# Two weight pieces loaded behind the first inputs, and a new order in the first slots, of an attention and two-layer kernel

## The chip, the cores and the metric

The kernel runs on one core of a Trainium2 chip. The metric is device time in microseconds (us) for one execution. TensorE (PE in the rows) multiplies, VectorE (DVE), ScalarE (ACT) and GpSimd (POOL) do elementwise work, SyncE (SP) issues nearly all transfers. TensorE's clock has two levels, 1.2 and 2.4 GHz; the rows give the granted share, 0.50 or 1.00.

## What is computed

Banded attention over 4 batches of 8 heads, then two feed-forward layers over 2304 tokens, all in float32. The layer weights come in as int64 views, of which the kernel makes float32 numbers.

```python
scores = scale * np.matmul(q, k.transpose(0, 1, 3, 2))
scores = np.where(masks[None, :, :, :], scores, -1000000000.0)
attn = np.exp(scores - np.max(scores, axis=-1, keepdims=True))
attn = attn / (np.sum(attn, axis=-1, keepdims=True) + 1e-09)
x = np.matmul(attn, v)            # then heads side by side: 2304 x 512
h = x @ w_in                      # first layer, 512 -> 2048
g = np.maximum(h, 0.0) + alpha * np.minimum(h, 0.0)
x = g @ w_out
h = x @ w_in2                     # second layer
g = np.where(h >= 1, h, np.where(h <= -1, 0.0, (h + 1) ** 2 / 4))
out = g @ w_out2
```

## The kernel before

**Splits.** Every product is made of three float32r matmuls: each operand is split into a high part (`hi`) and the rest (`lo`). `two` (lines 325 to 327) does it: ScalarE copies the high part (line 326), GpSimd or VectorE subtracts (line 327). The split of a w_in piece is called `wr`, that of a w_out piece `woh` and `wol`, that of x `xv`, that of g `gh` and `gl` (lines 660 and 666).

**Weight pieces.** A piece (layer, f, part) is one of 16 chunks f of w_in (part 0, tile `wi`) or w_out (part 1, `wo`; pieces that are kept for later are `wf`). `w_load` (line 271) loads 512 KB of it into a staging tile `st`, of which there are five. `w_make` turns it into float32 by three VectorE instructions (lines 320, 321 and 314), and when the third is done the staging tile is free for the next load. `conv(k)` hands out k of these instructions, so it says where they stand in VectorE's queue; `more` issues loads as long as a staging tile is free. `pend_l` and `pend_w` are the lists of pieces still to load and to make. `w_cut` splits each finished w_in piece.

**Attention.** 24 groups, six to a batch. The groups of batch 0 run ahead of everything, in a loop over i: scores (PE, lines 172 and 180), maximum and subtraction (DVE, lines 189 and 190), exp (ACT, line 192), a transpose of the previous group (line 211, evacuated as `pT`, line 213), its values (line 204), its normalisation (DVE, lines 228 to 230) and the output transpose of the one before (line 237, evacuated to `XA`, line 255). Groups 6 and up are spread over the slots of the first three tiles by `attention_point` (lines 141 to 164 for scores, 211 to 237 for the rest).

**Tiles and slots.** The first layer's tokens are tiles (0, 0) to (0, 3), the second layer's (1, 0) to (1, 2). Tiles (0, 0), (0, 1), (0, 2) and (1, 2) go in slots, one for each f: `f_h` makes h on TensorE (lines 513 to 515, twelve matmuls), `f_g` the activation (ACT line 650, DVE line 653, ACT line 660), `f_cut` the split of g, and `one_y` an earlier chunk's product with w_out into y (lines 688 to 690, twelve matmuls). h has two PSUM buffers, so h of chunk f + 2 needs that g of chunk f has been read. Slots are numbered by k from 0; the h of chunks 0 and 1 of tile (0, 0) stand between the last groups of batch 0, part by part, as x becomes ready.

**Pairs.** Tiles (0, 3), (1, 0) and (1, 1) have 1024 tokens and use Strassen's seven products. In the second half of such a tile, 16 steps of twelve matmuls each finish y for its second half of tokens, with `gx` loaded back from memory. Meanwhile `more_x` makes the next tile's seven inputs (22 operations of `x_seven`: sums called `room` on VectorE, and splits), `p_weights` the next tile's first weights (a split, four sums `ss`, further splits), and, in the first pair only, steps 3 to 10 make eight w_out pieces, three instructions each.

**What sets the order.** The order is written out by hand: each engine runs its instructions in the order in which the code issues them, and waits in that order.

Of the kernel before, what the change touches and what calls it, by code (L numbers as in the profile page):

```python
# [26 lines left out]
NF = DFF // P  # L27
# [31 lines left out]

EARLY = (3, 6)  # L60
READY = 12
# [26 lines left out]
def attention_then_two_ffns(ctx: ExitStack, tc: tile.TileContext, a0, aqk, av, w1i, w1o, w2i, w2o, alpha, masks, ident, out):  # L88
# [623 lines left out]
    with tc.manual_schedule(), ExitStack() as late:  # L712
# [22 lines left out]
        for i in range(NGB):  # L735
# [4 lines left out]
            if i == 1:  # L740
                nc.sync.dma_start(mask[:, 2 * GS:], masks[:, 2 * GS:])
        nc.sync.dma_start(al, alpha)
        nc.scalar.activation(half, half, AF.Exp, scale=0.0)
        nc.scalar.activation(half, half, AF.Copy, scale=0.5)
# [24 lines left out]
        def conv(k):  # L769

            for _ in range(k):
                if not todo and pend_w and pend_w[0] in cv:
                    todo.extend(w_make(*pend_w.pop(0)))
                if todo:
                    todo.pop(0)()
                    if not todo:
                        more()
# [8 lines left out]
        for i in range(NGB):  # L786
# [10 lines left out]
            w_cut()  # L797
            if i in FIRST:
                conv(3)
            if i == 3:  # L800
                x_split(n0, 0, True)

                nc.gpsimd.memset(qk[0], 0.0)
                hold = False
                a_load_qk(NGB)
                w_load(*pend_l.pop(0))
                w_load(*pend_l.pop(0))
                a_load_v(NGB)
                more()
# [17 lines left out]
        w_cut()  # L827
        conv(3)
        nc.vector.tensor_scalar(al, al, -1.0, 1.0, ALU.mult, ALU.add)
# [68 lines left out]
        def slot(n, f, k):  # L898
            nn = after_n[n]
            if k != 1:  # L900
                split_pending()
            w_cut()
            if n == LAST and f == NF - 1:
# [4 lines left out]
            if early:  # L908
                one_y()
            if n == PLAIN[0] and f == NF - 1:  # L910
                pend_l.extend(pend_2)
                pend_w.extend(pend_2)
# [8 lines left out]
            else:  # L921
                ops = 0
            attention_point()
            b0, b1 = BEFORE[n[0]]
            g = f_g(n, f, lambda: conv(min(ops, b0)))
            ops -= min(ops, b0)
            first_ops = min(ops, b1) if k else 1
            conv(first_ops)
            f_cut(n, f, g)
            if k == 0:  # L930
                wo_split((n, 0), f)
            w_cut()
            ahead = 2 if n == PLAIN[0] else 3
# [83 lines left out]
        for q, n in enumerate(PAIRS):  # L1017
# [41 lines left out]
            for i, f in enumerate(SECOND):  # L1059
# [12 lines left out]
                f_y((n, 1), f)  # L1072
                more_x(2)
                if nn in PAIRS:
# [122 lines left out]
```

## Time and profile before

| | us |
|---|---|
| median of three runs | 860.86 (858.82 to 861.88) |
| the profiled execution | 859.94 |
| its span | 858.2 |
| TensorE busy | 837.3 (98%) |
| VectorE busy | 554.5 (65%) |
| ScalarE busy | 428.8 (50%) |
| GpSimd busy | 481.9 (56%) |
| mean granted clock of TensorE | 0.992 |

The span is the time from the first to the last instruction of the profiled execution. In rows of the timeline, what stands in brackets at the end is how long the engine stood idle before the instruction, and which instruction's end released it. "issue" is a wait for nothing that the profile shows. An engine's busy time says little here of what bounds it: TensorE's idle time is 21 us in 858, and each piece of it stands in a place of its own.

### The profile page before, as it was taken

The numbers are of one execution on the slowest core, as the hardware profiler recorded it, in microseconds if no ns is written. First come the engines' busy times: TensorE is split into PE (matmuls) and PEld (weight loads), VectorE is DVE, ScalarE is ACT, GpSimd is POOL, SyncE is SP. The second block draws the span as 40 slices with busy tenths as digits, with TensorE's granted clock in tenths as the row PEclk, the third lists the DMA queues.
The fourth block names the chain that finished last, engine by engine and source line by source line (L and its number), as shares of the span: only waits on it lengthen the run. The fifth ranks groups of instructions, "written<-read, shape, count | busy, mean of one in ns | idle before, by whom it ended". The sixth has DMA issues, their size and how long they took to land.

```text
span 858.2 us, 14266 instructions
## 1 busy us (share of the span) xinstructions
PE 837.3 (98%) x5328; PEld 688.7 (80%) x5330; DVE 554.5 (65%) x911; ACT 428.8 (50%) x803; POOL 481.9 (56%) x411
## 2 busy tenths in 40 slices
PE   6899999999999999999998999999999999999998
PEld 4677777998777778888886888888888888888898
DVE  4788786666877576776678677776418677640143
ACT  3444444665534565555444556464335545453365
POOL 2365545777444677767346676763662332346486
PEclk8899999999999999999999999999999999999999
DMA  7787653764661025444287735333935553548220
GB/s 298 236 245 224 198 166 113 223 216 124 194 187 50 1 74 179 141 152 167 99 330 270 275 131 203 141 156 112 344 123 188 201 195 126 173 139 302 70 79 25
DMA packets 54980, 147.45 MB, mean 172 GB/s; under 512 B 5632, under 2 KB 13440, under 8 KB 54912
## 3 DMA queue, kind: packets, MB, share of 16 engines
q1 hardware_dynamic: 54624, 146.39, 50.3%
q8 instruction: 42, 0.69, 0.3%
q14 instruction: 26, 0.21, 0.1%
q10 hardware_dynamic: 288, 0.16, 0.1%
HBM read 101.97 MB, written 44.56 MB: 171 GB/s over the span
## 4 chain that ended last, share of the span: by engine, by line
PE 88%; DVE 6%; ACT 2%; issue 2%; DMA 1%; POOL 1%; SPq 0%; ACTq 0%; DVEq 0%
PE y L688 14%; PE y L690 14%; PE y L689 14%; PE h_ps L546 9%; PE h_ps L544 9%; PE h_ps L545 9%; PE h_ps L513 5%; PE h_ps L515 4%; PE h_ps L514 4%; PE o_ps L222 2%; PE s_ps L148 1%; DVE room L452 1%; PE t_ps L211 1%; PE x_ps L237 1%; DVE w_ps L321 1%
## 5 line engine op out<-in xcount | busy, mean ns | idle before, releaser
L327 POOL TENSOR_TENSOR wol<-wo,woh 128x512 fp32r<-128x512 f32 x153 | 200.0, 1314 | 86.5 <-ACT woh L326 86.2
L688 PE MATMUL y<-gh,wol 128*128 128x512 f32 (+1 forms) x444 | 164.0, 369 | 0.6 <-POOL wol L327 0.6
L690 PE MATMUL y<-gl,woh 128*128 128x512 f32 (+1 forms) x444 | 160.2, 361 | 0.0
L689 PE MATMUL y<-gh,woh 128*128 128x512 f32 (+1 forms) x444 | 160.2, 361 | 0.0
L327 POOL TENSOR_TENSOR wr<-wb,wr 128x512 fp32r<-128x512 f32 x60 | 77.7, 1295 | 128.3 <-ACT wr L326 128.3
L546 PE MATMUL h_ps<-xv,wr 128*128 128x512 f32 x336 | 130.8, 389 | 0.0
L545 PE MATMUL h_ps<-xv,wr 128*128 128x512 f32 x336 | 130.8, 389 | 0.0
L544 PE MATMUL h_ps<-xv,wr 128*128 128x512 f32 x336 | 130.7, 389 | 0.0
L326 ACT ACTIVATE woh<-wo 128x512 fp32r<-128x512 f32 x153 | 93.6, 626 | 71.8 <-PE y L690 52.2
L327 POOL TENSOR_TENSOR wr<-wi,wr 128x512 fp32r<-128x512 f32 x50 | 64.5, 1290 | 98.4 <-ACT wr L326 98.2
L688 PEld LDWEIGHTS y<-gh,wol 128*128 128x128 f32 x444 | 83.7, 189 | 16.7 <-POOL wol L327 2.3
L513 PE MATMUL h_ps<-xv,wr 128*128 128x512 f32 (+1 forms) x256 | 90.7, 354 | 3.8 <-DVE g L653 2.0
L690 PEld LDWEIGHTS y<-gl,woh 128*128 128x128 f32 x444 | 83.6, 188 | 13.4
L689 PEld LDWEIGHTS y<-gh,woh 128*128 128x128 f32 x444 | 83.8, 189 | 12.2
L514 PE MATMUL h_ps<-xv,wr 128*128 128x512 f32 (+1 forms) x256 | 87.0, 340 | 0.2 <-DVE xv L327 0.2
L515 PE MATMUL h_ps<-xv,wr 128*128 128x512 f32 (+1 forms) x256 | 87.0, 340 | 0.0
L558 ACT ACTIVATE g<-g,half 128x512 f32<-128x512 f32 x64 | 44.7, 723 | 72.1 <-DVE g L557 70.9
L688 PE MATMUL y<-gx,wol 128*128 128x512 f32 x192 | 75.5, 393 | 2.7 <-POOL wol L327 2.7
L689 PE MATMUL y<-gx,woh 128*128 128x512 f32 x192 | 75.3, 392 | 0.0
L690 PE MATMUL y<-gx,woh 128*128 128x512 f32 x192 | 75.3, 392 | 0.0
L545 PEld LDWEIGHTS h_ps<-xv,wr 128*128 128x128 f32 x336 | 63.1, 188 | 13.2
L544 PEld LDWEIGHTS h_ps<-xv,wr 128*128 128x128 f32 x336 | 63.1, 188 | 13.2
(122 smaller groups left out, 1513.7 us busy)
## 6 DMA issues: line engine op xcount, KB each, us to landing
gd<-XA SPq DMA_DIRECT2D x42, 512.0 KB, 3.5
gx<-gd SPq DMA_DIRECT2D x42, 512.0 KB, 5.9
wb<-whole SPq DMA_DIRECT2D x30, 512.0 KB, 4.8
st<-w1i SPq DMA_DIRECT2D x16, 512.0 KB, 5.0
st<-w1o SPq DMA_DIRECT2D x16, 512.0 KB, 5.2
st<-w2i SPq DMA_DIRECT2D x16, 512.0 KB, 4.8
st<-w2o SPq DMA_DIRECT2D x16, 512.0 KB, 4.8
kept<-wr SPq DMA_DIRECT2D x16, 512.0 KB, 2.7
```

Of the source, the lines that this page charges most:

```text
L326: nc.scalar.activation(hi, src, AF.Copy)
L327: low_on.tensor_tensor(lo, src, hi.bitcast(F32), ALU.subtract)
L513: nc.tensor.matmul(ps[:, :w], r[:, 1, cs], x[:, 0, xs], start=(c == 0), stop=False)
L514: nc.tensor.matmul(ps[:, :w], r[:, 0, cs], x[:, 1, xs], start=False, stop=False)
L515: nc.tensor.matmul(ps[:, :w], r[:, 0, cs], x[:, 0, xs], start=False, stop=(c == NC - 1))
L544: nc.tensor.matmul(o, w[:, 1, cs], x[:, 0], start=start and m == 0, stop=False, skip_group_check=not start)
L545: nc.tensor.matmul(o, w[:, 0, cs], x[:, 1], start=False, stop=False, skip_group_check=not start)
L546: nc.tensor.matmul(o, w[:, 0, cs], x[:, 0], start=False, stop=m == 1, skip_group_check=not start)
L558: nc.scalar.activation(t, t, AF.Square, bias=half, scale=0.5)
L688: nc.tensor.matmul(o, wl[:, cs], gh[:, :w], start=(i == 0), stop=False)
L689: nc.tensor.matmul(o, wh[:, cs], gh[:, :w], start=False, stop=False)
L690: nc.tensor.matmul(o, wh[:, cs], gl[:, :w], start=False, stop=(i == NF - 1))
```

## The change

Four things are moved; no instruction that computes is added or left out.

- The pieces (0, 2, 0) and (0, 0, 1) are loaded straight behind batch 0's inputs and alpha, ahead of the first transfers of batch 1 (`qk`, `vz`), and are made after the values of groups 3 and 4 (i = 4 and 5).
- In the first slots, VectorE's g of chunk 0 and 1 stands ahead of more of the pieces' instructions (`EARLY`, `b0`, `first_ops`); `w_cut` moves behind `f_g` in every slot of the plain tiles, and in slot 2 the split of the w_out piece stands behind the attention's instructions.
- The second layer's pieces are put on the list of loads two slots earlier, at f = 13 of tile (0, 0).
- In the second half of the first pair, the 22 input operations are given out as three in each of the first three steps, one in each of steps 3 to 10, and three after that, instead of two in each step.

```diff
--- before.py
+++ after.py
@@ -57,7 +57,7 @@
 
 FIRST = (0, 2)
 
-EARLY = (3, 6)
+EARLY = (2, 3)
 READY = 12
 BEFORE = ((1, 1), (1, 3))
 
@@ -740,6 +740,8 @@
             if i == 1:
                 nc.sync.dma_start(mask[:, 2 * GS:], masks[:, 2 * GS:])
         nc.sync.dma_start(al, alpha)
+        for _ in range(2):
+            w_load(*pend_l.pop(0))
         nc.scalar.activation(half, half, AF.Exp, scale=0.0)
         nc.scalar.activation(half, half, AF.Copy, scale=0.5)
         nc.gpsimd.memset(qk[1][:D, QK:], 0.0)
@@ -795,7 +797,7 @@
             if i >= 1:
                 e_values(i - 1)
             w_cut()
-            if i in FIRST:
+            if i in FIRST or i >= 4:
                 conv(3)
             if i == 3:
                 x_split(n0, 0, True)
@@ -803,8 +805,6 @@
                 nc.gpsimd.memset(qk[0], 0.0)
                 hold = False
                 a_load_qk(NGB)
-                w_load(*pend_l.pop(0))
-                w_load(*pend_l.pop(0))
                 a_load_v(NGB)
                 more()
             if i == 4:
@@ -825,7 +825,7 @@
         f_h(n0, 1, (2,))
         x_split(n0, 3)
         w_cut()
-        conv(3)
+        conv(1)
         nc.vector.tensor_scalar(al, al, -1.0, 1.0, ALU.mult, ALU.add)
         a_load_qk(NGB + 1)
         a_load_v(NGB + 1)
@@ -897,9 +897,10 @@
 
         def slot(n, f, k):
             nn = after_n[n]
-            if k != 1:
+            if k not in (1, 2):
                 split_pending()
-            w_cut()
+            if k > 1 and (n, f) not in wt:
+                w_cut()
             if n == LAST and f == NF - 1:
                 wo_split((n, 0), f)
             if k > 1 or n == LAST:
@@ -907,8 +908,9 @@
             early = f < 2 and k > 1
             if early:
                 one_y()
+            if n == PLAIN[0] and f == NF - 3:
+                pend_l.extend(pend_2)
             if n == PLAIN[0] and f == NF - 1:
-                pend_l.extend(pend_2)
                 pend_w.extend(pend_2)
             if n in PLAIN[:2] and f >= NF - NC:
                 x_split(nn, f - NF + NC, n == PLAIN[1])
@@ -921,15 +923,18 @@
             else:
                 ops = 0
             attention_point()
+            if k == 2:
+                split_pending()
             b0, b1 = BEFORE[n[0]]
-            g = f_g(n, f, lambda: conv(min(ops, b0)))
-            ops -= min(ops, b0)
-            first_ops = min(ops, b1) if k else 1
+            b0 = min(ops, b0) if k else 0
+            g = f_g(n, f, lambda: conv(b0))
+            ops -= b0
+            first_ops = min(ops, b1 if k else 3)
+            w_cut()
             conv(first_ops)
             f_cut(n, f, g)
             if k == 0:
                 wo_split((n, 0), f)
-            w_cut()
             ahead = 2 if n == PLAIN[0] else 3
             for i in range(1, ahead + 1):
                 if f + i < NF:
@@ -1070,7 +1075,7 @@
                         pend_y += [((n, 1), x) for x in SECOND[i:]]
                         break
                 f_y((n, 1), f)
-                more_x(2)
+                more_x(2 if q else 1 if 3 <= i < 11 else 3)
                 if nn in PAIRS:
                     if i in (5, 13):
                         w_base(nn[0], i // 13)
```

On VectorE, from the last split parts of group 5 to g of chunk 0 (line 653): `wi` is piece (0, 2, 0) before and (0, 3, 0) after, `wo` is (0, 0, 1) before and (0, 1, 1) after, `w_ps` the next piece in PSUM, `al` alpha. Before:

```order
L321 SCALAR_TENSOR_TENSOR wi<-st,wi 128x512
L314 SCALAR_TENSOR_TENSOR wi<-st,wi 128x512
L327 TENSOR_TENSOR xv<-XA,xv 128x512
L320 TENSOR_SCALAR wo<-st 128x512
L321 SCALAR_TENSOR_TENSOR wo<-st,wo 128x512
L314 SCALAR_TENSOR_TENSOR wo<-st,wo 128x512
L829 TENSOR_SCALAR al<-al 128x16
L320 TENSOR_SCALAR w_ps<-st 128x512
L653 SCALAR_TENSOR_TENSOR g<-g,al,h_ps 128x512
```

The same place after:

```order
L321 SCALAR_TENSOR_TENSOR wi<-st,wi 128x512
L314 SCALAR_TENSOR_TENSOR wi<-st,wi 128x512
L327 TENSOR_TENSOR xv<-XA,xv 128x512
L320 TENSOR_SCALAR wo<-st 128x512
L829 TENSOR_SCALAR al<-al 128x16
L653 SCALAR_TENSOR_TENSOR g<-g,al,h_ps 128x512
L321 SCALAR_TENSOR_TENSOR wo<-st,wo 128x512
```

Two instructions of the w_out piece and one of the next now stand behind g; the six of the two early pieces stand further up, between the normalisations of groups 3, 4 and 5.

On ScalarE, slots 0 and 1 of tile (0, 0), from gh of chunk 0 to pT of group 6. Before:

```order
L660 ACTIVATE gh<-g 128x512
L326 ACTIVATE woh<-wo 128x512
L326 ACTIVATE wr<-wi 128x512
L164 ACTIVATE s<-s 128x384
L650 ACTIVATE g<-h_ps 128x512
L660 ACTIVATE gh<-g 128x512
L326 ACTIVATE woh<-wo 128x512
L326 ACTIVATE wr<-wi 128x512
L213 ACTIVATE pT<-t_ps 128x384
```

After:

```order
L660 ACTIVATE gh<-g 128x512
L326 ACTIVATE woh<-wo 128x512
L164 ACTIVATE s<-s 128x384
L650 ACTIVATE g<-h_ps 128x512
L660 ACTIVATE gh<-g 128x512
L213 ACTIVATE pT<-t_ps 128x384
L326 ACTIVATE woh<-wo 128x512
```

Both splits of w_in pieces are gone from between, and pT stands ahead of the second woh.

On ScalarE, steps 8 and 9 of the first pair's second half (`wb` and `ss` are the next tile's weights and their sums). Before:

```order
L326 ACTIVATE woh<-wo 128x512 x2
L326 ACTIVATE xv<-room 128x512 x2
L326 ACTIVATE wr<-wb 128x512
L326 ACTIVATE woh<-wo 128x512
L326 ACTIVATE xv<-room 128x512
L326 ACTIVATE wr<-ss 128x512
```

After:

```order
L326 ACTIVATE xv<-XA 128x512
L326 ACTIVATE woh<-wo 128x512
L326 ACTIVATE wr<-wb 128x512
L326 ACTIVATE woh<-wo 128x512
L326 ACTIVATE wr<-ss 128x512
L326 ACTIVATE woh<-wo 128x512
```

The three splits of `room` no longer stand ahead of the weights' splits. TensorE's instructions stand in the same order before and after.

## Rows read from the trace of the kernel before

**Rows 1.** The page's first part: busy time, share of the span, instructions.

```profile
PE 837.3 (98%) x5328; PEld 688.7 (80%) x5330; DVE 554.5 (65%) x911; ACT 428.8 (50%) x803; POOL 481.9 (56%) x411
```

**Rows 2.** TensorE's timeline: start, duration, line, operation; in brackets the wait.

```profile
20.71 0.66 PE L204 MATMUL o_ps<-e_in,pT 64*32 64x65 f32 x25 [2.49 <-issue]
...
39.58 0.53 PE L513 MATMUL h_ps<-xv,wr 128*128 128x512 f32 x1 [1.95 <-DVE g L653]
...
48.69 0.87 PE L222 MATMUL o_ps<-vz,pT 128*32 128x130 f32 x24 [1.46 <-ACT pT L213]
...
149.99 0.39 PE L513 MATMUL h_ps<-xv,wr 128*128 128x256 f32 x1 [1.70 <-POOL wr L327]
...
272.35 0.55 PE L237 MATMUL x_ps<-idt,o 128*128 128x128 f32 x3 [0.55 <-DVE s L152]
...
279.61 0.87 PE L222 MATMUL o_ps<-vz,pT 128*32 128x130 f32 x24 [0.85 <-ACT pT L213]
...
464.81 0.50 PE L688 MATMUL y<-gx,wol 128*128 128x512 f32 x1 [2.30 <-POOL wol L327]
...
471.06 0.50 PE L688 MATMUL y<-gx,wol 128*128 128x512 f32 x1 [0.40 <-POOL wol L327]
```

**Rows 3.** Stretches: busy PE, PEld, DVE, ACT, POOL; granted clock, DMA share, GB/s.

```profile
14.00:16.00 2.00, 1.56 (x98) 1.23 (x97) 0.74 (x3) 0.34 (x1) 0.00 (x0) 0.99 1.03 405
20.00:22.00 2.00, 1.29 (x51) 0.82 (x59) 0.50 (x3) 1.30 (x4) 1.14 (x1) 0.50 0.05 8
40.00:42.00 2.00, 2.00 (x6) 1.56 (x5) 1.93 (x5) 0.90 (x3) 1.82 (x2) 0.50 1.00 318
46.00:48.00 2.00, 1.23 (x6) 0.69 (x4) 1.90 (x4) 0.39 (x2) 1.36 (x2) 1.00 1.01 281
```

**Rows 4.** TensorE's timeline: what follows h of chunk 2, and h of chunk 3.

```profile
44.00 0.49 PE L211 MATMUL t_ps<-idt,s 128*128 128x128 f32 x3
...
49.49 0.50 PE L513 MATMUL h_ps<-xv,wr 128*128 128x512 f32 x1
...
52.48 0.35 PE L141 MATMUL s_ps<-mask,idt 128*32 128x384 bf16 x4
```

**Rows 5.** VectorE's timeline, batch 0 to g of chunk 0.

```profile
16.09 0.42 DVE L320 TENSOR_SCALAR wi<-st 128x512 int32<-128x512 int32 x1
...
17.88 0.55 DVE L189 TENSOR_REDUCE mx<-s_ps 128x6 f32<-128x384 f32 x1
...
30.91 0.43 DVE L320 TENSOR_SCALAR wi<-st 128x512 int32<-128x512 int32 x1 [1.74 <-DMA st<-w1i]
...
35.13 1.52 DVE L320 TENSOR_SCALAR wo<-st 128x512 int32<-128x512 int32 x1
...
38.70 0.74 DVE L653 SCALAR_TENSOR_TENSOR g<-g,al,h_ps 128x512 f32<-128x512 f32 x1
```

**Rows 6.** The timelines of GpSimd (first row) and ScalarE in the same stretch.

```profile
35.08 1.28 POOL L327 TENSOR_TENSOR wr<-wi,wr 128x512 fp32r<-128x512 f32 x1 [7.85 <-ACT wr L326]
...
47.63 0.63 ACT L326 ACTIVATE wr<-wi 128x512 fp32r<-128x512 f32 x1 [1.61 <-DVE wi L314]
```

**Rows 7.** Transfers: packets of the instruction queue, 18.0 to 18.2 us; the load issued at 25.74.

```profile
q8 instruction: 1, 0.02, 34.7%
...
st<-w1i SPq DMA_DIRECT2D x1, 512.0 KB, 5.2
```

**Rows 8.** Timelines of SyncE and VectorE at the step to tile (0, 1).

```profile
140.36 1.48 SPq L271 DMA_DIRECT2D st<-w2i  x3
...
146.57 0.69 DVE L320 TENSOR_SCALAR w_ps<-st 128x512 int32<-128x512 int32 x1 [4.93 <-DMA st<-w2i]
```

**Rows 9.** Timelines of GpSimd and ScalarE in the first pair's second half.

```profile
455.05 1.29 POOL L327 TENSOR_TENSOR wol<-wo,woh 128x512 fp32r<-128x512 f32 x1 [0.72 <-ACT woh L326]
...
459.35 1.30 POOL L327 TENSOR_TENSOR wr<-wb,wr 128x512 fp32r<-128x512 f32 x1 [3.01 <-ACT wr L326]
...
457.66 1.09 ACT L326 ACTIVATE xv<-room 128x512 fp32r<-128x512 f32 x2 [2.69 <-DVE room L452]
```

## Prediction

> **What bounds the kernel now.** The page comes first: TensorE is busy for 98% of the span [rows 1]. The change leaves its instructions in the order they had, so only its waits, and matmuls at a low clock, can give anything back. Second, TensorE's own timeline, read for the rows that carry a wait: these eight are the larger ones after the first 18 us [rows 2]. Seven of them stand in four places that the change touches: the start of tile (0, 0) (39.58 and 48.69), the step to tile (0, 1) (149.99), the first steps of the Strassen inputs (272.35 and 279.61) and the second half of the first pair (464.81 and 471.06). Third, the stretches with their granted clock: the wait that ends at 39.58 is followed by a clock of 0.50, which is 1.2 GHz of 2.4, in 40 to 42 us, while the wait of 1.46 us that ends at 48.69 is not: 46 to 48 us stands at 1.00 with 1.23 of 2 us busy [rows 3]. Fourth, the queue of the engine that each wait names.
>
> **Start of tile (0, 0).** The kernel loses three amounts there.
>
> The first is the wait of 1.95 us: h of chunk 2 needs the PSUM buffer that VectorE's g of chunk 0 (line 653) frees, and that g starts at 38.70, behind pieces of weights in the same queue [rows 2, 5]. Of pieces, seven instructions stand ahead of g before: three of (0, 2, 0), three of (0, 0, 1), one of (0, 3, 0). Afterwards there are ten: the whole of (0, 3, 0), and the first of (0, 1, 1). A piece takes 1.79 us here (from 16.09 to 17.88), so three more instructions are 1.8 us. Against that, the first two pieces are loaded much earlier, in a stretch where the transfers stand nearly still (0.05 of the DMA engines busy, 20 to 22 us) [rows 3], so the wait of 1.74 us for the load at 30.91 goes; and L320 on `wo`, which took 1.52 us at 35.13 instead of 0.42, loses what held it, 1.1 us. Alone that would be 1.0 us in hand. But piece (0, 3, 0) now heads the queue in front of group 5's normalisation, as (0, 2, 0) did. Piece (0, 2, 0) landed 5.2 us after its issue at 25.74, so at 30.9 [rows 7]; (0, 3, 0) stands behind the same two qk transfers and also behind two vz transfers of 195 KB. These 0.4 MB take 1.0 us at the 405 GB/s of 14 to 16 us [rows 3], and longer in their rows of 1 KB; I estimate 1.6, so 32.5. VectorE was ready for that place at 29.2 (30.91 less 1.74); with two pieces ahead of it (3.6 us) it comes there at 32.8, or up to 1.1 us sooner by what they fill of its gaps between the last groups. So it waits up to 0.8 us for the load; I take 0.7 back, which leaves **0.3 us** of gain for this wait, with bounds of -0.8 (the 1.1 us of L320 comes again, now on piece (0, 1, 1) beside GpSimd's split of piece 3) and 1.0.
>
> About that L320: it began at 35.13, GpSimd's L327 ran from 35.08 for 1.28 us, and L320 ended when that was over [rows 5, 6]. The Trainium skill, page "SBUF — State Buffer", section "SBUF: two separate sides", states that VectorE in a 2-port mode and GpSimd take one port pair in turn and the later of the two blocks for the whole instruction; this row agrees. By it the two early pieces are safe only where GpSimd is idle, and the sum for this wait would be -0.8 instead of 0.3.
>
> The second is the clock. The twelve matmuls of h for chunk 2 take 4.42 us (39.58 to 44.00), those of chunk 3 take 2.99 (49.49 to 52.48) [rows 2, 4]. The change breaks the single wait of 1.95 into smaller ones earlier (TensorE waits for group 5's output, then for the third and fourth part of x). A wait of 1.46 us did not lower the clock [rows 3], so I expect it to stay: **1.43 us**; bounds 0 and 1.43.
>
> The third is the wait of 1.46 us at 48.69: pT of group 6 stands on ScalarE behind the split of piece 4 (47.63), which itself waited 1.61 us for VectorE [rows 2, 6]. In the new order pT stands ahead of both splits, and only gh of chunk 1 is before it. **1.46 us**; bounds 0.5 and 1.46. Its cover: y of chunk 0, twelve matmuls like an h, lies between the transposes and this place, so gh may come nearly 3 us late before it is felt.
>
> Together 3.2 us. The splits of `wi` that now stand behind relu and gh in each later slot cost nothing by this count: the split at 47.63 is of piece 4, while TensorE is at h of chunk 3 only at 49.49 [rows 4, 6].
>
> **Step to tile (0, 1).** VectorE waits 4.93 us for the first load of the second layer, until 146.57; its g for tile (0, 1) is queued behind that, gh and the two splits behind g, and TensorE waits 1.70 us [rows 2, 8]. The load is issued at 140.36 [rows 8]. The change asks for it two slots earlier. A slot holds an h and a y, twelve matmuls each, so two slots are nearly 12 us [rows 4]; with the 6.2 us from issue to use it lands near 135. The six instructions that slot 15 now adds on VectorE (about 0.69 us each, 4.1 us) fit the 4.93 us that it idled. I take **1.6 of 1.70**; bounds 0.5 and 1.7.
>
> **First steps of the Strassen inputs.** The second layer's pieces then end two pieces sooner, and two slots of tile (0, 2) lose three VectorE instructions each, some 2 us, ahead of what TensorE waits for at 272.35 (VectorE, 0.55) and 279.61 (ScalarE's pT, 0.85, itself behind VectorE's room) [rows 2]. TensorE too comes earlier by the first, so most of the second stays: **0.7**; bounds 0 and 1.4.
>
> **Second half of the first pair.** TensorE waits 2.30 us at 464.81 for wol of the twelfth step. GpSimd makes it last in a row that begins at 459.35: the split of the next pair's first weights, their four sums, then wol, 5.5 us until TensorE goes on. GpSimd had stood 3.01 us before that row, because ScalarE stood until 457.66, 2.69 us long, at splits of `room` that VectorE had not made: it was in a piece (three instructions per step) [rows 9]. The new distribution makes nine of the 22 input operations in the first three steps, when no piece is due, and one per step while pieces are made; then no split of `room` stands ahead of the weights on ScalarE. GpSimd can start the row when its wol of 455.05 is done, at 456.3, and end it at 461.8; TensorE is there at 462.5 (464.81 less 2.30). So 0.7 us are to spare. The 0.40 us at 471.06 is the tail of the same chain. **2.6 of 2.70**; bounds 0.4 and 2.7.
>
> **The sum.** 3.2 + 1.6 + 0.7 + 2.6 = 8.1 us. The profiled execution took 859.94 us, 858.2 of it span; 859.94 - 8.1 = 851.8. It lay 0.92 us below the median of the three runs shown (860.86), so on that scale it is 852.8. With every term at its better end: 1.0 + 1.43 + 1.46 + 1.7 + 1.4 + 2.7 = 9.7, so 851.2; the three runs spread 1.5 us about their middle, so the range opens at 850.2, a little below.
>
> **The rivals.** (1) *The wait is only moved.* VectorE stands at the load of (0, 3, 0) and the low clock comes after all; of the start 1.46 us remain, 6.4 in all: 854.5. For it: the same instruction waited 1.74 us before [rows 5]. Against: the two early pieces fall in idle transfers.
>
> (2) *GpSimd stays the bound in the pair.* The sums are in the same place, and only what ScalarE held back goes; 0.4 instead of 2.6 remain, 5.9 in all: 855.0. For: the thin reserve. Against: the 3.01 us that GpSimd stood [rows 9].
>
> (3) *The early loads delay TensorE's instructions.* At 20.71 TensorE resumes after 2.49 us in which it waited for nothing the profile shows, in the middle of a row of equal matmuls; one packet of the instruction queue shows at 18.0 us, when the inputs' transfers run out [rows 2, 7]. The change puts 1 MB behind those inputs, 2.6 us at the 405 GB/s of 14 to 16 us [rows 3]. If the packet comes out behind them, TensorE resumes 2.6 us later: 5.5 in all, 855.4. Against: the transfers were already full at 14 to 16 us, with megabytes queued, and the packet still came out. The Trainium skill, page "Runtime: NRT & Kernel Launch", section "Instruction fetch mechanics", calls the crossing of an instruction block mostly hidden; the 2.49 us here do not agree, and by that rule this rival would be worth nothing.
>
> (4) *Slower.* In the slots of tile (0, 0) the split of `wi` now stands behind relu and gh on ScalarE. If it then came too late in each of the 13 slots from chunk 3 on, TensorE would wait up to one split per slot, 0.63 on ScalarE and 1.28 on GpSimd [rows 6]: 13 x 1.91 = 24.8, less 8.1, so 16.7 us more than before: 877.6. From 0.62 us per slot on (8.1 / 13) it is slower than before. Against: pieces are a slot and more ahead [rows 4, 6].
>
> (5) *Nothing arrives*: each wait is replaced by a neighbour on the same engine: 859 to 861.
>
> **How the numbers follow.** Forecast (850.2 to 853.8) 0.50; rival 1 0.16, rival 2 0.12, rival 3 0.10, rival 4 0.05, rival 5 0.07. The range is to leave out no more than two in ten: it reaches over rivals 1 to 3 and a pair of them in part (two of them give about 857), so 850.2 to 857.0, with the forecast's own range inside. A measurement of this kernel can tell 0.3%, 2.6 us, from no change. Faster than 858.3: the forecast and rivals 1 to 3, 0.88; within: rival 5, 0.07; slower: 0.05.
>
> **What would show it.** Right: no TensorE wait over 1 us between 30 and 50 us and a granted clock of 1.00 in 38 to 44 us; o_ps of group 6 at about 45 instead of 48.69; no wait at the step to tile (0, 1), and VectorE's idle time for a load of the second layer gone; no wait for wol in the first pair. Wrong: a wait of VectorE for a load near 32 us with g of chunk 0 still near 38.7; TensorE resuming after 22 instead of 20.71; a wol wait of 1 us or more near 455 us; waits for wr in tile (0, 0).

## The result, and the profile after

The changed kernel takes 852.84 us (median of six executions; before 860.9 in the same measurement). The forecast was 852.8. One of the six took 1502.13 us at a mean granted clock of 0.769; it is left out of the ratio, 0.991 (95% interval 0.9895 to 0.9926), and without it the median is 852.67. The profile below is of another execution of the same kernel (852.03 us, span 850.2). Measured twice more, beside the experiments, the kernel took 853.15 us (ratio 0.9914, 0.9901 to 0.9926) and 852.38 us (0.9913, 0.9900 to 0.9927).

The page's first part, which answers to [rows 1]: TensorE is busy for 835.1 us, little less than the 837.3 of before. What the time lost is waits.

```profile
PE 835.1 (98%) x5330; PEld 687.4 (81%) x5330; DVE 557.2 (66%) x911; ACT 428.5 (50%) x803; POOL 483.3 (57%) x411
```

TensorE's timeline of the changed kernel, the rows that answer to [rows 2] and [rows 4] (start, duration, line, operation, and in brackets the wait):

```profile
20.69 0.43 PE L204 MATMUL o_ps<-e_in,pT 64*32 64x65 f32 x25 [2.07 <-issue]
...
30.07 0.55 PE L211 MATMUL t_ps<-idt,s 128*128 128x128 f32 x3 [1.01 <-ACT s L192]
...
35.33 0.52 PE L237 MATMUL x_ps<-idt,o 128*128 128x128 f32 x3 [1.66 <-DVE o L230]
...
40.29 0.47 PE L513 MATMUL h_ps<-xv,wr 128*128 128x512 f32 x1
...
43.15 0.55 PE L211 MATMUL t_ps<-idt,s 128*128 128x128 f32 x3
...
43.92 0.50 PE L688 MATMUL y<-gh,wol 128*128 128x512 f32 x1 [0.23 <-POOL wol L327]
...
46.87 0.87 PE L222 MATMUL o_ps<-vz,pT 128*32 128x130 f32 x24
...
274.99 0.87 PE L222 MATMUL o_ps<-vz,pT 128*32 128x130 f32 x24 [0.78 <-ACT pT L213]
...
298.79 0.50 PE L688 MATMUL y<-gh,wol 128*128 128x512 f32 x1 [0.57 <-POOL wol L327]
```

The waits at the step to tile (0, 1), at 272.35 and in the first pair are gone from the list; those for pT (now at 274.99) and for wol (298.79; before 0.58 us, at 303.45) stay nearly as they were. At the start, h of chunk 2 begins at 40.29, which is 0.71 us *later* than before, and TensorE's idle time now stands earlier, at 30.07 and 35.33.

The stretches around it (busy time of PE, PEld, DVE, ACT, POOL; granted clock; DMA share; GB/s), to be held against the 0.50 of [rows 3]:

```profile
38.00:40.00 2.00, 2.00 (x33) 1.38 (x33) 1.89 (x3) 0.60 (x1) 1.25 (x1) 1.00 0.84 275
40.00:42.00 2.00, 1.91 (x16) 1.43 (x9) 1.93 (x5) 1.15 (x2) 1.11 (x1) 1.00 1.03 254
```

VectorE and GpSimd in the changed kernel, 25 to 41 us, the rows that answer to [rows 5]:

```profile
25.35 1.52 DVE L320 TENSOR_SCALAR wi<-st 128x512 int32<-128x512 int32 x1
...
31.45 1.66 DVE L314 SCALAR_TENSOR_TENSOR wo<-st,wo 128x512 int32<-128x512 int32 x1
33.87 0.43 DVE L320 TENSOR_SCALAR wi<-st 128x512 int32<-128x512 int32 x1 [0.76 <-DMA st<-w1i]
...
38.02 1.26 DVE L829 TENSOR_SCALAR al<-al 128x16 f32<-128x16 f32 x1
39.40 0.75 DVE L653 SCALAR_TENSOR_TENSOR g<-g,al,h_ps 128x512 f32<-128x512 f32 x1
...
25.32 1.27 POOL L327 TENSOR_TENSOR xv<-XA,xv 128x512 fp32r<-128x512 f32 x1 [0.87 <-ACT xv L326]
...
31.00 1.56 POOL L327 TENSOR_TENSOR wr<-wi,wr 128x512 fp32r<-128x512 f32 x1 [4.40 <-ACT wr L326]
37.85 1.40 POOL L327 TENSOR_TENSOR wr<-wi,wr 128x512 fp32r<-128x512 f32 x1 [5.29 <-ACT wr L326]
```

Three times a VectorE instruction runs beside a cut on GpSimd, and each time it takes 1.0 to 1.1 us more than it does alone: 1.52 instead of 0.42 for L320, 1.66 instead of 0.69 for L314, 1.26 instead of 0.17 for the small L829. In all three the cut was already running, and what the VectorE instruction takes more is 0.14 us less than the cut still had to run. Before, this happened once [rows 5].

**A ladder of leads.** TensorE's matmuls stand in one order in before and after, and in all the experiments. So the start of the same matmul in two traces can be subtracted. The table gives, for six matmuls, the start before and by how much each kernel is ahead of it (us; a minus is behind). The columns are profiled executions; what each kernel is, the next section says. Three of the experiments' kernels, "late pieces", "late layer 2" and "cuts on VectorE", were traced twice; their columns are the second trace.

| matmul (start before) | after | early only | no start | late pieces | late layer 2 | no pair | cuts on VectorE |
|---|---|---|---|---|---|---|---|
| h, chunk 2 (39.58) | -0.71 | -1.08 | -0.34 | 0.56 | -0.64 | -0.78 | 0.63 |
| o_ps, group 6 (48.69) | 1.82 | 1.85 | -0.33 | 2.84 | 1.87 | 1.76 | 3.14 |
| y (59.60) | 1.86 | 1.27 | -0.34 | 1.69 | 1.91 | 1.79 | 3.17 |
| h, tile (0, 1) (149.99) | 3.98 | 2.04 | 1.52 | 3.81 | 2.81 | 3.92 | 5.31 |
| h (283.31) | 4.66 | 2.04 | 2.20 | 4.46 | 2.81 | 4.58 | 6.00 |
| h after the pair (473.93) | 7.90 | 1.90 | 5.47 | 7.76 | 6.06 | 3.12 | 9.16 |

So the changed kernel gains 1.86 at the start, 2.12 up to the first h of tile (0, 1) (0.25 of it by 134 us), 0.68 from there to 283 us and 3.24 after that, nearly all of it at the two waits for wol in the first pair; then the lead stays at 7.9 to the end.

### The profile page after: what moved, and what is told of

It is laid out like the page before. It is cut to its first block, busy times and chain, and to the rows that moved or that the text cites. A ratio compares the mean times of both kernels' runs of the same rounds, so it can differ in the third digit from the quotient of the medians.

```text
span 1500.3 us, 14285 instructions
## 1 busy us (share of the span) xinstructions
PE 1493.0 (100%) x5330; PEld 956.6 (64%) x5330; DVE 556.8 (37%) x911; ACT 436.5 (29%) x803; POOL 476.6 (32%) x411
## 4 chain that ended last, share of the span: by engine, by line
PE 99%; issue 0%; DVE 0%; DVEq 0%
PE y L688 16%; PE y L690 16%; PE y L689 16%; PE h_ps L546 9%; PE h_ps L545 9%; PE h_ps L544 9%; PE h_ps L513 6%; PE h_ps L514 6%; PE h_ps L515 6%; PE o_ps L222 2%; PE s_ps L148 2%; PE t_ps L211 1%; PE x_ps L237 1%; PE warm_ps L759 0%; PE o_ps L204 0%; PE s_ps L180 0%
## 5 line engine op out<-in xcount | busy, mean ns | idle before, releaser
L688 PE MATMUL y<-gh,wol 128*128 128x512 f32 (+1 forms) x444 | 255.7, 576 | 0.0
L690 PE MATMUL y<-gl,woh 128*128 128x512 f32 (+1 forms) x444 | 252.2, 568 | 0.0
L689 PE MATMUL y<-gh,woh 128*128 128x512 f32 (+1 forms) x444 | 251.3, 566 | 0.0
L544 PE MATMUL h_ps<-xv,wr 128*128 128x512 f32 x336 | 201.6, 600 | 0.0
L546 PE MATMUL h_ps<-xv,wr 128*128 128x512 f32 x336 | 201.5, 600 | 0.0
L545 PE MATMUL h_ps<-xv,wr 128*128 128x512 f32 x336 | 201.2, 599 | 0.0
L688 PEld LDWEIGHTS y<-gh,wol 128*128 128x128 f32 x444 | 120.0, 270 | 58.3 <-issue 43.7
L690 PEld LDWEIGHTS y<-gl,woh 128*128 128x128 f32 x444 | 123.0, 277 | 52.2 <-issue 39.2
L689 PEld LDWEIGHTS y<-gh,woh 128*128 128x128 f32 x444 | 121.2, 273 | 48.0 <-issue 35.1
L513 PE MATMUL h_ps<-xv,wr 128*128 128x512 f32 (+1 forms) x256 | 141.8, 554 | 0.0
L514 PE MATMUL h_ps<-xv,wr 128*128 128x512 f32 (+1 forms) x256 | 140.5, 549 | 0.0
L515 PE MATMUL h_ps<-xv,wr 128*128 128x512 f32 (+1 forms) x256 | 140.4, 549 | 0.0
L544 PEld LDWEIGHTS h_ps<-xv,wr 128*128 128x128 f32 x336 | 80.2, 239 | 56.0 <-issue 37.9
L545 PEld LDWEIGHTS h_ps<-xv,wr 128*128 128x128 f32 x336 | 79.9, 238 | 55.6 <-issue 36.7
L546 PEld LDWEIGHTS h_ps<-xv,wr 128*128 128x128 f32 x336 | 79.4, 236 | 56.3 <-issue 38.3
L690 PE MATMUL y<-gx,woh 128*128 128x512 f32 x192 | 110.8, 577 | 0.0
L689 PE MATMUL y<-gx,woh 128*128 128x512 f32 x192 | 110.4, 575 | 0.0
```

What stands on the lines that cost most here:

```text
L513: nc.tensor.matmul(ps[:, :w], r[:, 1, cs], x[:, 0, xs], start=(c == 0), stop=False)
L514: nc.tensor.matmul(ps[:, :w], r[:, 0, cs], x[:, 1, xs], start=False, stop=False)
L515: nc.tensor.matmul(ps[:, :w], r[:, 0, cs], x[:, 0, xs], start=False, stop=(c == NC - 1))
L544: nc.tensor.matmul(o, w[:, 1, cs], x[:, 0], start=start and m == 0, stop=False, skip_group_check=not start)
L545: nc.tensor.matmul(o, w[:, 0, cs], x[:, 1], start=False, stop=False, skip_group_check=not start)
L546: nc.tensor.matmul(o, w[:, 0, cs], x[:, 0], start=False, stop=m == 1, skip_group_check=not start)
```

## The experiments

Each run is given with its median and its ratio to the kernel before, which was timed beside it on the same chip. Three groups of four runs were made; the kernel before took 860.49, 860.05 and 859.88 us in them.

### The changed kernel as yardstick

> The changed kernel once more, for a profile that can be laid beside that of before. By the terms of the prediction its span is 8.1 us under the 858.2 of before, about 850: TensorE's h of chunk 2 at about 39.3 instead of 39.58 at a granted clock of 1.00 (so the transposes behind it near 42.3 instead of 44.00), o_ps of group 6 near 45.3 without a wait, no wait over 0.2 us at the step to tile (0, 1), one of the two waits of the Strassen inputs left (0.7), none for wol in the first pair. By rival 1 the clock is 0.50 around 40 us; by rival 2 a wait for wol of about 2 us is left; by rival 3 TensorE resumes at 23 instead of 20.71.

> The changed kernel once more, as the yardstick on this chip: 852.6 to 853.3; TensorE 1.8 us ahead of before at 60 us, no wait at 150 us, clock 1.00 in 38 to 44 us.

Measured: 853.15 and 852.38 us. In the second trace h of chunk 2 is 0.62 us late and the lead at 59.60 is 1.90, so the rows above hold in another execution.

### The pair alone undone

```
-                more_x(2 if q else 1 if 3 <= i < 11 else 3)
+                more_x(2)
```

> The changed kernel with two input operations in every step of the first pair's second half, as before. If that part is worth its term, this is 2.6 us slower than the changed kernel (0.4 to 2.7) and its profile has the waits of 2.3 and 0.4 us for wol again; if GpSimd is the bound there in either order (rival 2), it is within 0.5 us of the changed kernel.

Measured: 855.93 us (0.9949, 0.9935 to 0.9964), 2.78 us above the changed kernel. The waits for wol are back, and GpSimd again stands for 3 us ahead of the row of sums, as in [rows 9]. TensorE and GpSimd of this kernel:

```profile
461.69 0.50 PE L688 MATMUL y<-gx,wol 128*128 128x512 f32 x1 [2.40 <-POOL wol L327]
...
467.95 0.50 PE L688 MATMUL y<-gx,wol 128*128 128x512 f32 x1 [0.45 <-POOL wol L327]
...
456.23 1.30 POOL L327 TENSOR_TENSOR wr<-wb,wr 128x512 fp32r<-128x512 f32 x1 [3.10 <-ACT wr L326]
```

And GpSimd of the changed kernel at the same place:

```profile
450.41 1.30 POOL L327 TENSOR_TENSOR wol<-wo,woh 128x512 fp32r<-128x512 f32 x1 [1.45 <-ACT woh L326]
451.67 1.29 POOL L327 TENSOR_TENSOR wr<-wb,wr 128x512 fp32r<-128x512 f32 x1
...
456.28 1.30 POOL L327 TENSOR_TENSOR wol<-wo,woh 128x512 fp32r<-128x512 f32 x1
```

The split of the next weights follows the wol ahead of it at once, as the prediction said. The new distribution is shown to be what removes this wait. (The ladder of this kernel loses more than that, since the profiled execution is the slowest of its four: it falls back by 1.4 us between 340 and 400 us, most of it at one more wait, of 0.69 us at 379.40, which the last section takes up.)

### The second layer's loads at their old slot

```
-            if n == PLAIN[0] and f == NF - 3:
-                pend_l.extend(pend_2)
             if n == PLAIN[0] and f == NF - 1:
+                pend_l.extend(pend_2)
                 pend_w.extend(pend_2)
```

> The changed kernel with the second layer's loads put on the list at f = 15 again. By the terms of the prediction 1.6 us for the step to tile (0, 1) and 0.7 us for the Strassen inputs come back, 2.3 us in all (0.5 to 3.1), with VectorE's wait of some 5 us for the load and TensorE's of 1.7 us for wr in the profile. If the loads do not matter there, it is the same as the changed kernel.

> The changed kernel with the second layer's loads at their old slot, once more, beside the changed kernel itself: by the traces' rows 1.0 us at the step to tile (0,1) (wait of 0.87 and the restart) and 0.6 to 0.7 us before 284 us, 1.6 to 2.0 us above the changed kernel in all; by the medians so far 0.7 us. A wait of 0.4 to 1.0 us for wr near 147 us if the rows hold in other executions.

Measured: 853.88 us (0.9925, 0.9911 to 0.9939) and 853.90 us (0.9927, 0.9914 to 0.9939), 0.73 and 1.52 us above the changed kernel. In the traces the difference at 283 us is 2.0 (first pair of runs) and 1.9 (second: a lead of 2.81 against 4.69). TensorE and VectorE in the second of them:

```profile
147.18 0.39 PE L513 MATMUL h_ps<-xv,wr 128*128 128x256 f32 x1 [1.10 <-POOL wr L327]
...
269.55 0.55 PE L237 MATMUL x_ps<-idt,o 128*128 128x128 f32 x3 [0.56 <-DVE s L152]
...
276.80 0.87 PE L222 MATMUL o_ps<-vz,pT 128*32 128x130 f32 x24 [0.87 <-ACT pT L213]
...
143.75 0.70 DVE L320 TENSOR_SCALAR w_ps<-st 128x512 int32<-128x512 int32 x1 [3.98 <-DMA st<-w2i]
```

VectorE stands for the load again (3.98 us; 4.93 in [rows 8]) and TensorE waits at the step, but for 0.87 and 1.10 us in the two traces, not 1.70. The waits of 0.55 and 0.85 us near 272 and 279 us are back whole. So the rest of the change shortens the step's wait by itself, and the earlier loads remove what is left of it, and the wait for s at 272.35. The first 0.25 us of the step's gain comes before the load is needed (by 134 us) and is there in this kernel too. The medians give the earlier loads less than the traces do; nine and ten executions of the two kernels overlap (852.3 to 854.6 and 852.0 to 853.4), and I leave it at 0.7 to 2.0 us.

In the changed kernel SyncE issues that load at 125.20, and VectorE does not wait for it:

```profile
125.20 5.68 SPq L271 DMA_DIRECT2D st<-w2i  x3
...
139.79 0.69 DVE L320 TENSOR_SCALAR w_ps<-st 128x512 int32<-128x512 int32 x1
```

### The start undone: no early pieces, old order in the slots

The loads and pieces stand at their old places, and the body of the slot is that of before.

```
-EARLY = (2, 3)
+EARLY = (3, 6)
...
-        for _ in range(2):
-            w_load(*pend_l.pop(0))
...
-            if i in FIRST or i >= 4:
+            if i in FIRST:
...
-            b0 = min(ops, b0) if k else 0
-            g = f_g(n, f, lambda: conv(b0))
-            ops -= b0
-            first_ops = min(ops, b1 if k else 3)
-            w_cut()
+            g = f_g(n, f, lambda: conv(min(ops, b0)))
+            ops -= min(ops, b0)
+            first_ops = min(ops, b1) if k else 1
```

> The kernel before with the two other parts alone (second layer's loads earlier, new distribution in the first pair), the start as before. By the terms it is 3.2 us slower than the changed kernel (1.5 to 4.8), 4.9 us faster than before, with h of chunk 2 at 39.58, a clock of 0.50 in 40 to 42 us and the wait of 1.46 us for pT. By rival 1 it is only 1.5 us slower than the changed kernel.

Measured: 854.87 us (0.9944, 0.9926 to 0.9962), 1.72 us above the changed kernel. All that before shows at this place is back (TensorE, and the stretch with its clock of 0.58):

```profile
39.92 0.47 PE L513 MATMUL h_ps<-xv,wr 128*128 128x512 f32 x1 [1.93 <-DVE g L653]
...
49.02 0.87 PE L222 MATMUL o_ps<-vz,pT 128*32 128x130 f32 x24 [1.44 <-ACT pT L213]
...
40.00:42.00 2.00, 2.00 (x6) 1.56 (x7) 1.97 (x4) 0.95 (x2) 1.49 (x2) 0.58 0.98 330
```

So the whole start is worth 1.7 us by the medians, not 3.2; the two traces differ by 2.2 at 59.60, of which 0.3 stands already at 20.7 us, ahead of all that was moved on VectorE. It has two parts, the early pieces and the order in the slot, and the next two runs take them apart.

### The early pieces alone

The kernel before with the two early loads and pieces, and nothing else of the change. `EARLY` stays at (3, 6), so slots 0 and 1 hand out nine instructions of pieces where the changed kernel hands out five.

```
         nc.sync.dma_start(al, alpha)
+        for _ in range(2):
+            w_load(*pend_l.pop(0))
...
-            if i in FIRST:
+            if i in FIRST or i >= 4:
                 conv(3)
...
-                w_load(*pend_l.pop(0))
-                w_load(*pend_l.pop(0))
...
-        conv(3)
+        conv(1)
         nc.vector.tensor_scalar(al, al, -1.0, 1.0, ALU.mult, ALU.add)
```

> The kernel before with the early pair of pieces alone: loads behind batch 0's inputs, pieces made at groups 4 and 5; the slots, the second layer's loads and the pair as before. Theory A (the early pieces alone carry the start's gain): by the group at 60 us TensorE is 1.2 to 1.9 us ahead of before, the granted clock in 40 to 44 us is 1.00, the wait of 1.70 us at 150 us stays, as do those at 272 and 465 us; 858.6 to 859.3 against 860.5 (ratio 0.998). Theory B (the new order in the first slots carries it): clock near 0.55 in 40 to 44 us, the pT wait of about 1.4 us near 48 us stays, no gain. Rival 3 of the prediction (the early loads delay TensorE's instruction packet): TensorE resumes after 22 us, slower than before by about 1 us.

Measured: 858.34 us (0.9977, 0.9966 to 0.9988), 1.7 us below before. TensorE is 1.85 us ahead at o_ps of group 6; 0.6 of it goes by 60 us, and the wait at the step to tile (0, 1) falls by 0.47:

```profile
147.95 0.39 PE L513 MATMUL h_ps<-xv,wr 128*128 128x256 f32 x1 [1.23 <-POOL wr L327]
```

Theory A's first half holds: by themselves the early pieces bring some 1.7 us. In the trace 1.27 of it are there by 59.60, although TensorE resumes 0.52 us later at 21.23 than before does at 20.71, which may hold some of it back. The 0.47 at the step is time that the earlier loads of the second layer clear in the changed kernel anyway. Whether the four more instructions of pieces in slots 0 and 1 take the 0.6 us was not tried.

### The order in the slots without the early pieces

The changed kernel with the loads and the pieces at their old places.

```
-EARLY = (2, 3)
+EARLY = (3, 6)
...
-        for _ in range(2):
-            w_load(*pend_l.pop(0))
...
-            if i in FIRST or i >= 4:
+            if i in FIRST:
                 conv(3)
...
-        conv(1)
+        conv(3)
         nc.vector.tensor_scalar(al, al, -1.0, 1.0, ALU.mult, ALU.add)
```

> The changed kernel without the early pieces (loads and pieces at their old places), with the new order in the slots, the second layer's earlier loads and the pair. Theory A: TensorE is within 0.4 us of before at 60 us, clock near 0.55 in 40 to 44 us, no wait at 150 us, then 0.7 and 3.2 us from the Strassen inputs and the pair: 6 us ahead at the end, about 854.6, within 0.5 us of the run without the whole start. Theory B: 1.5 us or more of the start's gain is there, 853.2.

> The changed kernel with the early pair of pieces back at its old place, once more, beside the changed kernel itself. Theory C (early pieces and new slot order remove the same lost time, each alone is enough): within 0.6 us of the changed kernel. Theory D (they add): 1.3 to 1.9 us above it. On the clock: if the idle time of 1.6 us before chunk 2 is what lowers it, it is near 0.55 in 40 to 44 us in this execution, with the start's gain then near zero; the last execution of this kernel had that idle time and 1.00.

Measured: 852.83 us (0.9913, 0.9892 to 0.9934), and, with the changed kernel beside it, 852.32 us (0.9910, 0.9897 to 0.9924) against its 852.38. Theory A falls in its second half: without the early pieces nothing is lost that the medians show, so with the new order in place the early pieces bring no more (theory C). The other direction is shown less well: the early pieces alone bring 1.27 us of the start in their trace, and no kernel had them and the other two parts without the new order. The two executions of the late pieces also differ: the lead at 59.60 is 0.92 in the first and 1.69 in the second. TensorE, VectorE and ScalarE of the second run, and the stretch:

```profile
39.02 0.47 PE L513 MATMUL h_ps<-xv,wr 128*128 128x512 f32 x1 [1.44 <-DVE g L653]
...
50.26 0.35 PE L141 MATMUL s_ps<-mask,idt 128*32 128x384 bf16 x4 [0.58 <-DVE o L230]
...
31.26 0.43 DVE L320 TENSOR_SCALAR wi<-st 128x512 int32<-128x512 int32 x1 [2.31 <-DMA st<-w1i]
...
38.13 0.75 DVE L653 SCALAR_TENSOR_TENSOR g<-g,al,h_ps 128x512 f32<-128x512 f32 x1
38.79 0.69 DVE L320 TENSOR_SCALAR w_ps<-st 128x512 int32<-128x512 int32 x1
...
44.91 0.47 ACT L213 ACTIVATE pT<-t_ps 128x384 f32<-128x384 f32 x1
...
40.00:42.00 2.00, 2.00 (x9) 1.31 (x7) 1.93 (x5) 0.07 (x1) 2.00 (x2) 1.00 0.95 282
```

VectorE still stands for the load (2.31 us, more than the 1.74 of before), and h of chunk 2 still waits for g (1.44). But in the first slot the order puts L320 on w_ps behind g, where it stood ahead before: g starts at 38.13 instead of 38.70. And pT of group 6 begins at 44.91 (48.16 before), so its wait is gone. The clock stays at 1.00 after this idle time, as it did in the first run after 1.57 us; it fell to 0.50 and 0.58 after the 1.95 of before and the 1.93 of the kernel without the start. That the length decides does not follow: in before, the wait of 2.30 us that ends at 464.81 leaves the clock at 1.00:

```profile
464.00:466.00 2.00, 1.19 (x5) 1.00 (x6) 1.63 (x3) 1.87 (x4) 1.86 (x2) 1.00 0.87 260
```

### The moved first instruction, and the cuts on VectorE

If the early pieces bring nothing beside the new order because VectorE runs into GpSimd, taking that collision away must show it. The first kernel only moves one instruction, so that group 4's outputs don't queue behind the load that lands at 33.8:

```
-        conv(1)
         e_values(NGB - 1)
+        conv(1)
         x_split(n0, 2)
```

> The changed kernel with one edit: the first instruction of the third early-side piece stands behind group 4's values on VectorE instead of ahead of them, so that group 4's outputs no longer queue behind a load that has not landed (VectorE idle 0.76 us at 33.87 us, and the instruction's 0.42 us). If VectorE's lateness sets the start: TensorE's wait of 1.66 us for o at 35.3 us falls to 0.5 to 0.9, chunk 2 starts 0.5 to 1.0 us earlier than at 40.29, time 0.7 below the changed kernel (852.4). Rival: GpSimd's cuts (gl, wol) are next at once: the wait of 0.23 us for wol at 43.9 grows by as much, time unchanged (853.1).

Measured: 852.40 us (0.9908, 0.9892 to 0.9925), 7.65 us below before, where the changed kernel is 7.34 and 7.50 below. That is no difference this measurement can tell. The wait for o is 0.48 instead of 1.66, but part of that is chance: TensorE comes to it 0.7 us later in this execution, and in the changed kernel's second trace the wait is 1.04. The matmul behind it begins 0.48 us earlier, and the lead at 59.60 only grows from 1.86 to 2.05: TensorE meets the next row of the same VectorE queue (0.27 us for xv at 37.63). The rival comes nearer, though its own row (wol, 0.23) has not grown. TensorE of this kernel:

```profile
34.85 0.52 PE L237 MATMUL x_ps<-idt,o 128*128 128x128 f32 x3 [0.48 <-DVE o L230]
...
43.73 0.50 PE L688 MATMUL y<-gh,wol 128*128 128x512 f32 x1 [0.23 <-POOL wol L327]
```

The second kernel adds that the three cuts run on VectorE, between its own instructions:

```
-        two(t[:, 0], t[:, 1], wi[n[0], f], nc.vector if n == PAIRS[0] and f < 2 else nc.gpsimd)
+        two(t[:, 0], t[:, 1], wi[n[0], f], nc.vector if n == PAIRS[0] and f < 2 or n == order[0] and f in (2, 3) else nc.gpsimd)
...
-            w_cut()
+            if i < NGB - 1:
+                w_cut()
...
-                x_split(n0, 1, True)
+                x_split(n0, 1)
...
-        w_cut()
         conv(1)
+        w_cut()
         nc.vector.tensor_scalar(al, al, -1.0, 1.0, ALU.mult, ALU.add)
```

> As the run before it in this list, and the three low parts that GpSimd cuts at 25.3, 31.0 and 37.9 us are cut by VectorE, between its own instructions. If the two engines block each other there: VectorE's instructions of 1.52, 1.66 and 1.26 us fall to 0.43, 0.69 and 0.17, for three more of 0.69, so VectorE gains 1.10+0.97+1.09-3 x 0.69 = 1.1 us beside the 0.76; chunk 2 starts near 38.8 to 39.3 instead of 40.29 and the time is 851.3 to 852.2. Rival 1: gains on VectorE are eaten by GpSimd's later cuts (853). Rival 2: VectorE now has the cuts in its queue ahead of scores and waits for ScalarE's high parts: slower than the changed kernel by up to 1 us (854).

> The three cuts on VectorE and the moved first instruction, once more, beside the changed kernel itself: 1.3 to 2.0 us below it (851.0 to 851.6), TensorE 2.7 to 3.1 us ahead of before at 60 us, no VectorE instruction over 0.8 us between 24 and 40 us.

Measured: 851.30 us (0.9894, 0.9879 to 0.9910), and beside the changed kernel 850.64 us (0.9891, 0.9877 to 0.9904), 1.74 below its 852.38; the two ranges, 850.40 to 850.94 and 851.97 to 853.38, do not meet. This version beats both kernels. The moved first instruction is part of it; beside the kernel that has only that one, in the same group, the cuts are worth 1.1 us (851.30 against 852.40, ranges 850.98 to 851.56 and 851.90 to 853.26). VectorE and GpSimd of the second run:

```profile
26.03 0.42 DVE L320 TENSOR_SCALAR wi<-st 128x512 int32<-128x512 int32 x1
...
31.55 0.69 DVE L314 SCALAR_TENSOR_TENSOR wo<-st,wo 128x512 int32<-128x512 int32 x1
32.16 0.68 DVE L327 TENSOR_TENSOR wr<-wi,wr 128x512 fp32r<-128x512 f32 x1
...
37.46 0.17 DVE L830 TENSOR_SCALAR al<-al 128x16 f32<-128x16 f32 x1
38.07 0.75 DVE L653 SCALAR_TENSOR_TENSOR g<-g,al,h_ps 128x512 f32<-128x512 f32 x1 [0.43 <-ACT g L650]
...
39.56 1.74 POOL L666 TENSOR_TENSOR gl<-g,gh 128x512 fp32r<-128x512 f32 x1 [15.08 <-ACT gh L660]
```

The three long instructions take 0.42, 0.69 and 0.17 us again, though VectorE now does three more of 0.68 to 0.69. g starts at 38.07 instead of 39.40, and there it waits for ScalarE, not for VectorE's own queue. h of chunk 2 is 0.63 us ahead of before instead of 0.71 behind.

## Why the prediction was right, point by point

**The total.** 8.1 us were forecast; 7.3 and 7.5 were measured against the kernel before of the same group (8.1 in the first measurement), and the profiled executions differ by 7.9. The places were right. The terms were off in both directions, and the errors cancelled: in the ladder the start gave 1.3 us less than forecast, the stretch up to tile (0, 1) 0.5 more and the pair 0.6 more. That the median met the forecast to 0.1 us is luck.

**Start of tile (0, 0): 3.2 forecast, 1.9 in the trace, 1.7 by the run without it.** The failing step is the wait for g. The prediction took +0.3 and named -0.8 as the bound, for the case that L320's 1.1 us come again beside GpSimd's split; the trace gives -0.71. The third overlap, 1.26 instead of 0.17 us right ahead of g, is the one of that bound. But there were three, and the load was late too. The third piece's first instruction starts at 33.87, where the load lands (issued at 28.08, 5.8 us before); the prediction had the load at 32.5. The first two overlaps, 2.1 us, stand ahead of that; without them VectorE would have waited that much longer for the load, or nearly so (in the second trace it gets there at 33.66 and does not wait). The step's sum also has a slip: VectorE waits up to 0.8 us for the load only if it comes up to 1.1 us sooner, and that time is not credited. By the prediction's own numbers the third piece starts at 32.5 to 32.8 and g is 1.0 to 1.3 earlier than before, so the step missed by 1.7 to 2.0 us; 1.1 to 1.4 of it are the late start of the third piece, the rest comes behind it, where the third overlap stands.

The step should have laid GpSimd's three cuts beside VectorE's row, since all three stood in the instruction order. The Trainium skill, page "SBUF — State Buffer", section "SBUF: two separate sides", on the port that the two engines take in turn, is borne out by these rows and by the run with the cuts on VectorE. The sum by it (-0.8) came nearer for this wait, though it counted one overlap and met the number by chance.

The clock term is right for the changed kernel: h of chunk 2 takes 2.86 us (40.29 to 43.15) instead of 4.42, 1.56 where 1.43 was forecast. But its reason is only half right: the run without the early pieces keeps the clock too, with the single idle time still there, 1.44 and 1.57 us long. The pT term is right in its mechanism (pT at 44.94, o_ps without a wait) and off in size: 0.97 of 1.46 reach o_ps, since y of chunk 0 now waits for wol and restarts.

**What carries the start.** The prediction gave the g wait and the clock to the early pieces and pT to the order in the slots. The runs show substitutes, in the main: early pieces alone 1.7 (1.27 of it by 59.60), order alone as much as both. Adding the terms as if each edit had its own was wrong, though the true value lies within the bounds of the start (-0.3 to 3.9).

**Step to tile (0, 1): 1.6 forecast, 1.87 in the trace** (from 134 to 150 us). Right in size, and the load alone is enough: with the start undone the lead still grows from -0.33 to 1.52 there. But again the parts overlap: without that load the wait is 0.87 to 1.10 us, not 1.70, and with the early pieces alone it is 1.23. What upstream shortens it was not separated.

**First steps of the Strassen inputs: 0.7 forecast, 0.68 in the ladder.** The wait for s at 272.35 is gone and the one for pT at 279.61 stays (0.78 of 0.85), as forecast. With the second layer's loads late both are back, so the earlier loads are the cause. The way is the one given: VectorE's last piece of this stretch begins at 253.85 instead of 273.40.

**First pair: 2.6 forecast, 2.78 measured, 3.24 in the ladder.** Mechanism and place right. The ladder gives more than the 2.70 of waits that [rows 2] show: each of these two waits costs 0.27 us more from start to start than its bracket says. At 464.81 the start before is at 462.12 and the next one at 465.15; with a regular step of 0.23 that is 2.46 and 0.11 us, 2.57 for a bracket of 2.30.

**The rivals.** Rival 1 (the wait is only moved) is half true: the idle time does stand earlier, at 30.07 behind VectorE's late s and at 35.33 behind its late o, and VectorE stands for the load (0.76 at 33.87), but the clock stays at 1.00. Rival 2 is out: GpSimd's row starts without a gap. Rival 3 is out: TensorE resumes at 20.69 and 20.97 us in the two traces (20.71 before), and the packet begins at 18.19 and 18.48 (18.17 before), so it does not come out behind the early loads. Rival 4 is out: there is no wait for wr in tile (0, 0). Rival 5 is out by the interval.

**The signs named.** As forecast: the clock, no wait at the step, none for wol in the pair. Not as forecast: TensorE waits of 1.01 and 1.66 us that end within 30 to 50 us, g of chunk 0 at 39.40 behind a wait for a load (the mark for wrong was "near 38.7"), and o_ps of group 6 at 46.87, where 45 was the mark. By its own sign the prediction was wrong on the g wait.

## What to carry to other kernels

Two edits that remove the same idle time are not worth their sum: undo each by itself before crediting it. When work is moved into a gap of VectorE, lay GpSimd's instructions of that stretch beside it; here three VectorE instructions took about 1 us more each, and moving the three cuts onto the busier engine was 1.1 us faster. A wait's price is read from the starts around it, not from its bracket.

## What the runs showed of the hardware

- A VectorE instruction on 128x16 elements (0.17 us alone) took 1.26 us beside a GpSimd cut. GpSimd's cut was longer too, 1.56 and 1.40 us against 1.27.
- TensorE's stop near 18 to 21 us, with no releaser in the profile, ends between 20.68 and 21.24 in all thirteen traces, whatever its length: waits of 1.80, 2.07, 2.49 and 3.08 us end at 20.68, 20.69, 20.71 and 20.71 in four kernels. What it follows is the packet of the instruction queue [rows 7]: the packet begins at 18.17 to 18.80 us, and TensorE resumes 1.27 to 1.48 us after the packet's end in each of the thirteen. No run moved the packet, so that it is the cause is not shown.
- The clock does not follow the idle time in any simple way. Before chunk 2 it stayed at 1.00 after 1.44 and 1.57 us and fell after 1.93 and 1.95, but near 465 us it stayed at 1.00 after 2.30 us. Nor did it fall after the 1.66 us that end at 35.33 in the changed kernel. A wait of a given length has no fixed price in clock; why it fell at one place alone stays open.
- In three of the thirteen traces TensorE waits once between 340 and 400 us for a second-layer piece of VectorE (wf, line 314), for 0.81, 0.69 and 0.20 us, in three different kernels, one of which shows no such wait in its second trace. Its cause stays open, as does the spread of the kernel before, 858.82 to 861.88 us.
